# First head pairs of an attention + two-MLP kernel: who issues which load, k ahead of q, weight loads later, and w3 transposed as fp32r

## The chip, the cores and the metric

One core of a Trainium2 chip runs the kernel. The metric is device microseconds of one launch, the median of several runs.

## What is computed

Three stages in fp32, one after the other (cut from the reference; every weight is an input):

```python
# attention: q, k, v are (4, 8, 576, 64)
def rotate(x):
    x1, x2 = (x[..., :half], x[..., half:])
    return np.concatenate([x1 * cos - x2 * sin, x1 * sin + x2 * cos], axis=-1)
scores = scale * np.matmul(rotate(q), rotate(k).transpose(0, 1, 3, 2))
attn = softmax(scores)                 # max subtracted, 1e-09 added to the sum
x = np.matmul(attn, v)                 # then heads are merged: (2304, 512)

# first MLP: d_ff 1536
xn = x / rms * rms_g
x = (silu(xn @ w_gate) * (xn @ w_val)) @ w_out

# second MLP: d_ff 1024
h = (x @ w1) * (x @ w2) @ w3
out = h @ w_out2
```

## The kernel before, in words

Precision is kept by splitting: an fp32 value becomes a high part of type fp32r and a low part (value minus high part, also fp32r), and a product of two such values is three fp32r matmuls. ScalarE (ACT) makes the high part with a copy, VectorE (DVE) or GpSimd (POOL) subtracts it from the value for the low part.

**Attention** runs over 16 pairs of heads. For a pair, `load` (line 494) brings q and k into a tile `raw` of nine blocks per head: blocks 0 to 3 are q's rows 0 to 511, blocks 4 to 7 k's, block 8 holds the last 64 rows of both. `ra`, `rb`, `rc`, `rd` (lines 532 to 558) do the rotation: times cosine, the two half products with the sine (`rb` needs the negated sine, which ACT makes at line 880), and the sum, into `rot`. GpSimd does it for all pairs but the first, where VectorE does blocks 4 to 7 and 0 to 3 and GpSimd block 8. Three groups of transposes follow, `q2p` (k's blocks), `q1p` (q's) and `q0p` (block 8), line 591; for each, `q?h` copies the high part and `q?l` subtracts the low part into the tile `xy` (lines 595, 600). From `xy`, DMAs fill the stacks that the score matmuls read: `q2d` fills `ks` with four transfers (288 KB each), `q1d` fills `qs` with four (160 KB each), both through `move` (line 612). For the first pair part of the stacks is filled by copies and subtracts on the engines (lines 602, 889, 901).

A pair then goes through nine tiles of 128 query rows: `S` scores (line 660), `M` row maximum (665), `E` exponential (671), `T` transpose of the probabilities (677), `H` and `Lo` their split (681, 685), `LP`, `LH`, `LL` the same for the leftover columns (707, 711, 715), then `PV` (733), `OS` (738), `O` (747) and the scaled result `X`.

The order is written out by hand. `ORDER` gives each step a place inside a pair, in units of a ninth of a pair; pair p adds 9p; steps whose names begin with `q` or `v` are those of the next pair, and `ra` to `rd`, `lq`, `lv` those of the pair after it. `ONCE` gives single places: `WF.n` issues the load of weight unit n (512 KB, lines 405 and 407), `W0.n` to `W5.n` convert it (`W0` is an ACT instruction on the loaded tile, line 430; `W1` a DVE one, line 434). All steps are sorted by place, and each engine runs its own in that order, so an instruction that waits holds up all that follow it on its engine. DMAs are issued by SP (SyncE), in the same way in order. `WARM` counts filler transposes of the identity `idn` (line 877) between the first pair's transposes.

**The MLPs** are laid out by `Plan` (line 129): each operation has an estimated duration, operands and engine, and TensorE's order is the order of the program. `w3_trans(j)` (line 1541) transposes a part of w3, eight transposes of 128x128 for each of eight j, in two groups of four with a planned duration of 0.44; `w3_prod` multiplies the transposed part with the second `w_out`. Lines of other large products: 1305, 1452, 1561, 1619.

Of the kernel before, what the change touches and what calls it, by code (L numbers as in the profile page):

```python
# [30 lines left out]

ONCE = {"WF.0": 0.058, "WF.1": 0.481, "W0.0": 2.871, "W1.0": 9.2, "W2.0": 9.7, "W0.1": 7.205, "W3.0": 10.2,
# [8 lines left out]
WARM = (22, 18, 3, 26)  # L41
SEGS = ((0, 0, 4), (1, 0, 12), (0, 4, 12))
# [35 lines left out]
PRI = 100  # L78
Q_LATE = 0.023
LGROUPS = ((0, 1, 2, 3), (4,), (5, 6, 7, 8))  # L80
# [193 lines left out]
def kernel(  # L274
# [63 lines left out]

    idn = const.tile([128, 128], F32, name="idn")
    g_sb = const.tile([128, DM], F32, name="g")  # L340
# [153 lines left out]
    def load(p, t=None):  # L494
        raws[p] = t = raw_p.tile([128, 2, 9, D], F32, tag="raw", name="raw") if t is None else t
        nc.sync.dma_start(out=t[:, :, 4:8, :].rearrange("p h r d -> p h (r d)"), in_=main(k, p))
        if p == 0:
            nc.sync.dma_start(out=sin_sb[:, 1], in_=sin_t)
        nc.sync.dma_start(out=t[:, :, 0:4, :].rearrange("p h r d -> p h (r d)"), in_=main(q, p))
        if p == 0:  # L500
            nc.sync.dma_start(out=cos_sb[:, 0:4], in_=cos_t[:, 0:4])
        nc.sync.dma_start(out=t[64:128, :, 8, :], in_=left(k, p))
        nc.sync.dma_start(out=t[0:64, :, 8, :], in_=left(q, p))

# [77 lines left out]
    def qt(g):  # L582

        n = [1, 4, 4][g]
        r0 = [8, 0, 4][g]
        c = slice(*((0, 512) if g == 1 else (QW + LF, QW + S)))

        def qp(p):
            ps = ps_g.tile([128, 512], F32, tag="g", name="qtp")
            for i in range(n):  # L590
                nc.tensor.transpose(ps[:, i * 128:(i + 1) * 128], rots[p][:, r0 + i].rearrange("p h d -> p (h d)"), idn)  # L591
            qps[p, g] = ps if g else ps[:, 0:128].rearrange("p (a b) -> p a b", a=2)

        def qh(p):
            nc.scalar.copy(out=xs[:, c] if g else two(xs), in_=qps[p, g])

        def ql(p):
            hi, lo = (xs[:, c], ys[:, c]) if g else (two(xs), two(ys))
            ps = qps.pop((p, g))
            nc.vector.tensor_tensor(out=lo, in0=ps, in1=f(hi), op=ALU.subtract)  # L600
            if p == 0 and g == 1:
                nc.vector.tensor_tensor(out=qst[0][64:128, 0, 0:512], in0=ps[0:64], in1=f(hi)[0:64], op=ALU.subtract)

        for n_, fn in (("p", qp), ("h", qh), ("l", ql)):
            part[f"q{g}{n_}"] = fn
# [8 lines left out]
    @step  # L614
    def q1d(p):
        qs = qst[p % 2]
        sl = slice(0, 640)
        sa = sl
        if p == 0:
            sa = slice(512, 640)  # L620
        move([(qs[0:64, 0, sa], xs[0:64, sa]), (qs[64:128, 0, sa], ys[0:64, sa]),
              (qs[64:128, 1, sl], xs[64:128, sl]), (qs[0:64, 1, sl], ys[64:128, sl])])

    @step
    def q2d(p):
        new_ks(p)
        ks = stacks[p]
        sl = slice(QW, QW + S)
        move([(ks[a:a + 64, 2 * h:2 * h + 2], xy[64 * h:64 * h + 64, :, sl]) for h in range(p == 0, 2) for a in (0, 64)])

# [228 lines left out]
    nc.vector.memset(eps, 1e-9)  # L859
    make_identity(nc, idn)  # L860
    man = ExitStack()
    man.enter_context(tc.manual_schedule())
    nc.sync.dma_start(out=cos_sb[:, 4:9], in_=cos_t[:, 4:9])
    load(0)
# [15 lines left out]
    nc.scalar.mul(out=sin_sb[:, 0], in_=sin_sb[:, 1], mul=-1.0)  # L880
    for n, eng in ((slice(4, 8), nc.vector), (slice(8, 9), nc.gpsimd), (slice(0, 4), nc.vector)):
        for n_ in ("ra", "rb", "rc", "rd"):
            part[n_](0, eng, n)
    for n_ in ("ra", "rb", "rc", "rd"):
        part[n_](1)
    new_ks(0)

    def k_copy(eng, i, r):
        eng(out=stacks[0][r:r + 64, i], in_=xy[0:64, i, QW:QW + S])

    for i, n_ in enumerate(("q2p", "q0p", "q1p")):
        part[n_](0)
        warm(i + 1)
    for n_ in ("q2h", "q0h", "q2l", "q0l", "q2d"):
        part[n_](0)
    k_copy(nc.scalar.copy, 0, 0)
    for r in (0, 64):
        k_copy(nc.vector.tensor_copy, 1, r)
    part["q1h"](0), part["q1l"](0)
    k_copy(nc.scalar.copy, 0, 64)  # L900
    nc.scalar.copy(out=qst[0][0:64, 0, 0:512], in_=xs[0:64, 0:512])
    for n_ in ("q1d", "vh", "vl"):
# [801 lines left out]
```

## Time and profile before

| | us |
|---|---|
| median of 3 runs | 1057.66 (1057.07 to 1058.37) |
| the profiled execution | 1058.29 |
| its span, first to last instruction | 1056.4 |
| TensorE busy in it | 1039.7 (98%) |
| DVE, ACT, POOL busy | 782.3, 646.3, 356.2 |

The span is what the views below show; the profiled execution's time is 1.9 us more, which lies around the span. In the views PE is TensorE, PEld its weight loads, SPq the queue of SP. A busy PE may run at half clock: PEclk says what was granted, 1.00 for 2.4 GHz and 0.50 for 1.2.

### The profile page before, as it was taken

To read this page: it belongs to the slowest core of one execution; us is meant where nothing else is said; L and a number is where in the kernel's file an instruction comes from. 1 tells how busy PE (TensorE), PEld (TensorE's weight loads), DVE (VectorE), ACT (ScalarE), POOL (GpSimd) and SP (SyncE) were. 2 spreads that over 40 slices of the span, in tenths; PEclk is the share of its full clock that TensorE was granted. 3 is DMA by queue.
4 is the path that set the end of the run, shared out by engine and by line. 5 is a ranking of instruction groups with operands and counts; after the bars stand their busy time and mean duration, and the time that the engine had idled before them with its cause. 6 is when DMAs were issued, how large, how long until landed. Compare 5 with 4: busy or idle time off the path is not lost.

```text
span 1056.4 us, 19366 instructions
## 1 busy us (share of the span) xinstructions
PE 1039.7 (98%) x6849; PEld 1024.1 (97%) x6849; DVE 782.3 (74%) x1382; ACT 646.3 (61%) x1433; POOL 356.2 (34%) x479
## 2 busy tenths in 40 slices
PE   8899999999999999999999999999999999999998
PEld 7799999999999999999999999999999999989998
DVE  7899999999987965878787777443675574774663
ACT  5799999899977655457666675422554444454330
POOL 7779788889610002532222230001521110000000
PEclk9999999999999999999999999999999999999999
DMA  7778876768669876369988967561352326751751
GB/s 197 163 204 204 223 184 177 195 184 197 175 212 307 284 259 231 95 213 341 312 299 266 310 231 233 166 214 48 107 205 81 125 76 214 276 197 53 269 217 61
DMA packets 124864, 211.36 MB, mean 200 GB/s; under 512 B 19040, under 2 KB 71776, under 8 KB 123232
## 3 DMA queue, kind: packets, MB, share of 16 engines
q1 hardware_dynamic: 124768, 210.14, 63.8%
q8 instruction: 54, 0.88, 0.3%
q14 instruction: 42, 0.34, 0.1%
HBM read 117.62 MB, written 63.96 MB: 172 GB/s over the span
## 4 chain that ended last, share of the span: by engine, by line
PE 94%; DVE 2%; DMA 2%; POOL 1%; issue 1%; SPq 0%; ACT 0%; DVEq 0%; POOLq 0%
PE ps L1305 33%; PE ps L1452 9%; PE mm L1062 9%; PE ps L1619 9%; PE s L660 7%; PE pv L733 7%; PE tp L677 6%; PE acc L1088 5%; PE ps L1561 4%; PE lp L707 1%; PE op L747 1%; PE qtp L591 1%; DMA ks<-xy 1%; PE ps L1548 1%; PE xp L1189 1%; DMA raw<-in_q_dram 1%
## 5 line engine op out<-in xcount | busy, mean ns | idle before, releaser
L995 DVE TENSOR_TENSOR v<-v 128x256 fp32r<-128x256 f32 (+7 forms) x436 | 277.5, 666 | 115.1 <-ACT v L989 103.0
L1305 PE MATMUL ps<-v 128*128 128x384 f32 x2016 | 350.0, 334 | 0.0
L1305 PEld LDWEIGHTS ps<-v 128*128 128x128 f32 x2016 | 349.4, 188 | 0.0
L989 ACT CAST v<-v 128x256 fp32r<-128x256 f32 (+4 forms) x372 | 196.0, 556 | 149.4 <-PE ps L1305 38.8
L995 POOL TENSOR_TENSOR v<-v 128x256 f32<-128x256 f32 (+1 forms) x120 | 113.7, 963 | 427.6 <-DMA v<-wsG 159.6
L995 DVE TENSOR_TENSOR v<-ps,v 128x384 f32<-128x384 f32 (+3 forms) x154 | 84.3, 567 | 86.4 <-PE ps L1305 46.7
L989 ACT COPY v<-ps 128x384 f32<-128x384 f32 (+1 forms) x126 | 60.2, 478 | 113.0 <-PE ps L1305 57.0
L660 PE MATMUL s<-ks,qs 128*128 128x288 f32 x640 | 120.4, 314 | 7.2 <-DMA ks<-xy 3.1
L665 DVE TENSOR_REDUCE nm<-s 128x1 f32<-128x576 f32 x144 | 108.0, 750 | 11.4 <-PE s L660 9.7
L671 ACT ACTIVATE p<-s,nm 128x576 f32<-128x576 f32 x144 | 107.4, 746 | 11.2 <-DVE nm L665 10.5
L1062 PE MATMUL mm<-v 128*128 128x384 f32 x576 | 104.2, 335 | 0.1
L1062 PEld LDWEIGHTS mm<-v 128*128 128x128 f32 x576 | 99.9, 188 | 0.4 <-DVE pt L685 0.4
L1452 PE MATMUL ps<-v 128*128 128x384 f32 x576 | 100.0, 334 | 0.0
L1452 PEld LDWEIGHTS ps<-v 128*128 128x128 f32 x576 | 99.9, 188 | 0.0
L660 PEld LDWEIGHTS s<-ks,qs 128*128 128x128 f32 x640 | 89.9, 190 | 9.9 <-issue 4.9
L685 DVE TENSOR_TENSOR pt<-tp,pt 128x512 fp32r<-128x512 f32 x144 | 94.7, 682 | 1.2 <-ACT pt L681 0.6
L1619 PEld LDWEIGHTS ps<-v 128*128 128x128 f32 x756 | 90.9, 192 | 0.1
L1619 PE MATMUL ps<-v 128*128 128x256 f32 x756 | 90.9, 283 | 0.0
L677 PE MATMUL tp<-idn,p 128*128 128x128 f32 x576 | 82.7, 276 | 1.5 <-DVE x L773 0.7
L681 ACT CAST pt<-tp 128x512 fp32r<-128x512 f32 x144 | 82.3, 585 | 1.5 <-PE tp L677 0.7
L733 PE MATMUL pv<-pt,vs 128*128 128x288 f32 x512 | 80.9, 300 | 0.1
L677 PEld LDWEIGHTS tp<-idn,p 128*128 128x128 f32 x576 | 68.1, 142 | 3.5 <-PE s L660 1.3
(118 smaller groups left out, 1262.0 us busy)
## 6 DMA issues: line engine op xcount, KB each, us to landing
ks<-xy SPq DMA_DIRECT2D x62, 288.0 KB, 4.9
v<-in_moe_w_dram SPq DMA_DIRECT2D x32, 512.0 KB, 6.0
v<-uD SPq DMA_DIRECT2D x12, 1344.0 KB, 7.3
v<-in_moe_w_out_dram SPq DMA_DIRECT2D x20, 512.0 KB, 6.4
qs<-xy SPq DMA_DIRECT2D x62, 160.0 KB, 2.8
uG<-v SPq DMA_DIRECT2D x24, 384.0 KB, 4.1
v<-uG SPq DMA_DIRECT2D x24, 384.0 KB, 3.7
uD<-v SPq DMA_DIRECT2D x12, 768.0 KB, 3.6
```

The source lines that it names most:

```text
L660: nc.tensor.matmul(ps[:, hf, 0:HS], lhsT=l, rhs=r_[:, hf * HS:(hf + 1) * HS], start=(i == 0), stop=(i == n - 1))
L665: nc.vector.tensor_reduce(out=nm, in_=s_ps[p, t][:, :, 0:HS], axis=AX.XY, op=ALU.max, negate=True)
L671: nc.scalar.activation(out=pp.rearrange("p (a b) -> p a b", a=2), in_=s_ps.pop((p, t))[:, :, 0:HS], func=AF.Exp, bias=s_max.pop((p, t)), s ...
L677: nc.tensor.transpose(ps[:, c, :], p_sb[p, t][:, LF + c * 128:LF + (c + 1) * 128], idn)
L685: lastins["dve"] = nc.vector.tensor_tensor(out=lo, in0=src, in1=f(hi), op=ALU.subtract)
L733: nc.tensor.matmul(ps[:, 0:HS], lhsT=l.rearrange("p s d -> p (s d)"), rhs=r, start=(i == 0), stop=(i == 8))
L989: return plan("ACT", act_us(n), lambda: nc.scalar.copy(out=o(), in_=i()), rd, wr)
L995: lambda: eng.tensor_tensor(out=o(), in0=x(), in1=y(), op=op), rd, wr)
L1062: nc.tensor.matmul(p_, lhsT=w.ap[:, a, s, c * 128:(c + 1) * 128], rhs=x.ap[:, b_, c, :], start=(j == 0), stop=(j == 3 * KC - 1))
L1305: nc.tensor.matmul(p_(), lhsT=w[i].ap[:, a, c * 128:(c + 1) * 128], rhs=x[i].ap[:, r, c], start=(first and ch != 1 and n == 0), stop=(n == 5),
L1452: nc.tensor.matmul(ac[o][ch][0](), lhsT=w.ap[:, a, o * 128:(o + 1) * 128], rhs=u.ap[:, b_, ch], start=(j == 0 and s == 0), stop=(j == NF - ...
L1619: nc.tensor.matmul(p_()[:, k * 256:(k + 1) * 256], lhsT=u.ap[:, a, UOP[i], o * 128:(o + 1) * 128], rhs=w.ap[:, b_], start=(g == 0 and s == ...
```

## The change

- Opening loads. The first half of the cosines that is needed, the sine, and the first pair's two 64-row pieces are issued by ACT instead of SP. SP issues the first pair's k, then q, then the rest of the cosines, and for the second pair k, the two pieces, then q.
- The identity is made in a scratch tile and copied by ACT into an fp32r tile `idr`; `idn` is the fp32 view of it.
- First pair: the rotation's order is `ra`, `rc`, `rb`, `rd`. k's low part is subtracted from PSUM directly into both halves of the stack (`k_lo`), for the 512 main columns and the 64 left ones apart; the high part is copied there by ACT (`k_hi`). The DMAs to the other head's stack are split in the same way (`k_move`), and the last DMAs to `qs` are issued in another order. `WARM` has smaller numbers.
- Second pair: GpSimd rotates blocks 4 to 8 first, then 0 to 3. Its `q2` and `q0` steps stand ahead of S2 and near S3 of the first pair, with `q2d` ahead of E2; its `q1` steps stand at 1.2 to 1.42.
- The first two weight loads move from 0.058 and 0.481 to 1.6 and 1.7, and `W0.0` from 2.871 to 5.8.
- `w3_trans` transposes as fp32r, with `idr`.

```diff
-ONCE = {"WF.0": 0.058, "WF.1": 0.481, "W0.0": 2.871, "W1.0": 9.2, "W2.0": 9.7, "W0.1": 7.205, "W3.0": 10.2,
+ONCE = {"WF.0": 1.6, "WF.1": 1.7, "W0.0": 5.8, "W1.0": 9.2, "W2.0": 9.7, "W0.1": 7.205, "W3.0": 10.2,
-WARM = (22, 18, 3, 26)
+WARM = (20, 15, 3, 16)
-Q_LATE = 0.023
+FIRST = {"q2p": -0.34, "q0p": -0.335, "q2h": -0.2, "q0h": -0.19, "q2l": -0.06, "q0l": -0.05, "q2d": -0.03,
+    "q1p": 1.2, "q1h": 1.25, "q1l": 1.4, "q1d": 1.42}
...
-    idn = const.tile([128, 128], F32, name="idn")
+    idr = const.tile([128, 128], F32R, name="idr")
+    idn = f(idr)
...
     def load(p, t=None):
+        first = p == 0
+        if first:
+            nc.scalar.dma_start(out=cos_sb[:, 4:9], in_=cos_t[:, 4:9])
         nc.sync.dma_start(out=t[:, :, 4:8, :].rearrange("p h r d -> p h (r d)"), in_=main(k, p))
-        if p == 0:
-            nc.sync.dma_start(out=sin_sb[:, 1], in_=sin_t)
-        nc.sync.dma_start(out=t[:, :, 0:4, :].rearrange("p h r d -> p h (r d)"), in_=main(q, p))
-        if p == 0:
+        if first:
+            nc.scalar.dma_start(out=sin_sb[:, 1], in_=sin_t)
+        if p != 1:
+            nc.sync.dma_start(out=t[:, :, 0:4, :].rearrange("p h r d -> p h (r d)"), in_=main(q, p))
+        if first:
             nc.sync.dma_start(out=cos_sb[:, 0:4], in_=cos_t[:, 0:4])
-        nc.sync.dma_start(out=t[64:128, :, 8, :], in_=left(k, p))
-        nc.sync.dma_start(out=t[0:64, :, 8, :], in_=left(q, p))
+        eng = nc.scalar if first else nc.sync
+        eng.dma_start(out=t[64:128, :, 8, :], in_=left(k, p))
+        eng.dma_start(out=t[0:64, :, 8, :], in_=left(q, p))
+        if p == 1:
+            nc.sync.dma_start(out=t[:, :, 0:4, :].rearrange("p h r d -> p h (r d)"), in_=main(q, p))
...
-make_identity(nc, idn)
+ident = p_p.tile([128, S], F32, tag="p", name="ident")[:, 0:128]
+make_identity(nc, ident)
+nc.scalar.copy(out=idr, in_=ident)
-nc.sync.dma_start(out=cos_sb[:, 4:9], in_=cos_t[:, 4:9])
...
-    for n_ in ("ra", "rb", "rc", "rd"):
-        part[n_](1)
+    for n in (slice(4, 9), slice(0, 4)):
+        for n_ in ("ra", "rb", "rc", "rd"):
+            part[n_](1, nc.gpsimd, n)
...
+    def k_lo(c, r):
+        src = qps[0, 2] if c is K_MAIN else qps[0, 0][:, 1, 0:64]
+        nc.vector.tensor_tensor(out=ks[r:r + 64, 1, c[0]:c[1]], in0=src[0:64], in1=f(xs)[0:64, QW + c[0]:QW + c[1]], op=ALU.subtract)
...
-    for i, n_ in enumerate(("q2p", "q0p", "q1p")):
+    for i, n_ in enumerate(("q2p", "q1p", "q0p")):
         part[n_](0)
         warm(i + 1)
-    for n_ in ("q2h", "q0h", "q2l", "q0l", "q2d"):
+    ps_k = qps[0, 2]
+    part["q2h"](0)
+    for r in (0, 64):
+        k_hi(K_MAIN, r)
+    nc.vector.tensor_tensor(out=ys[:, QW + LF:QW + S], in0=ps_k, in1=f(xs)[:, QW + LF:QW + S], op=ALU.subtract)
+    k_move(K_MAIN)
+    for r in (0, 64):
+        k_lo(K_MAIN, r)
+    part["q1h"](0)
+    part["q0h"](0)
+    nc.scalar.copy(out=qst[0][0:64, 0, 0:512], in_=xs[0:64, 0:512])
+    nc.vector.tensor_tensor(out=qst[0][64:128, 0, 0:512], in0=qps[0, 1][0:64], in1=f(xs)[0:64, 0:512], op=ALU.subtract)
+    for r in (0, 64):
+        k_hi(K_LEFT, r)
+        k_lo(K_LEFT, r)
+    for n_ in ("q0l", "q1l"):
         part[n_](0)
-    k_copy(nc.scalar.copy, 0, 0)
-    for r in (0, 64):
-        k_copy(nc.vector.tensor_copy, 1, r)
-    part["q1h"](0), part["q1l"](0)
-    k_copy(nc.scalar.copy, 0, 64)
-    nc.scalar.copy(out=qst[0][0:64, 0, 0:512], in_=xs[0:64, 0:512])
+    k_move(K_LEFT)
...
-                at(9 * p + t + (Q_LATE if p == 0 and n_[0] == "q" else 0), part[n_], p + d)
+                at(9 * p + (FIRST.get(n_, t) if p == 0 else t), part[n_], p + d)
...
-                    nc.tensor.transpose(p_()[:, c * 128:(c + 1) * 128], src.ap[:, c * 128:(c + 1) * 128], idn)
+                    nc.tensor.transpose(p_()[:, c * 128:(c + 1) * 128].bitcast(F32R), src.ap[:, c * 128:(c + 1) * 128].bitcast(F32R), idr)
```

## Rows read from the trace of the kernel before

**Rows 1.** The page: busy time and share by engine; shares of the chain that ended last.
```profile
PE 1039.7 (98%) x6849; PEld 1024.1 (97%) x6849; DVE 782.3 (74%) x1382; ACT 646.3 (61%) x1433; POOL 356.2 (34%) x479
...
PE 94%; DVE 2%; DMA 2%; POOL 1%; issue 1%; SPq 0%; ACT 0%; DVEq 0%; POOLq 0%
```

**Rows 2.** Stretches: length, busy us of each engine, granted clock, DMA share, GB/s.
```profile
20.00:30.00 10.00, 8.07 (x59) 7.10 (x59) 9.04 (x15) 9.30 (x24) 10.00 (x15) 1.00 0.99 248
...
29.00:32.00 3.00, 0.04 (x1) 0.00 (x0) 0.54 (x1) 1.68 (x4) 2.42 (x3) 1.00 1.05 231
...
34.00:36.00 2.00, 2.00 (x11) 1.98 (x11) 1.44 (x2) 1.49 (x5) 0.23 (x1) 0.50 1.02 322
...
40.00:44.00 4.00, 3.69 (x30) 3.28 (x30) 4.00 (x8) 3.13 (x7) 4.00 (x4) 1.00 0.20 45
44.00:50.00 6.00, 5.44 (x43) 5.18 (x43) 5.94 (x10) 4.85 (x13) 5.93 (x9) 1.00 0.82 180
...
50.00:100.00 50.00, 50.00 (x411) 49.75 (x410) 48.96 (x87) 47.11 (x117) 39.09 (x57) 1.00 0.81 205
...
890.00:960.00 70.00, 70.00 (x370) 62.12 (x369) 53.15 (x92) 37.22 (x70) 0.00 (x0) 1.00 0.55 199
```

**Rows 3.** Order of time, opening: start, us, engine, line, operation [idle before <-releaser].
```profile
0.74 1.28 ACT L871 ACT_TABLE_LOAD   x1 [0.74 <-PEq L1690]
...
1.36 4.77 PE L877 MATMUL warm<-idn 128*128 128x128 f32 x22 [1.36 <-POOL idn masks.py:199]
...
3.95 0.62 SPq L503 DMA_DIRECT2D raw<-in_q_dram  x1
...
10.87 2.37 DVE L889 CAST ks<-xy 64x576 fp32r<-64x576 f32 x2
...
14.83 1.28 PE L660 MATMUL s<-ks,qs 128*128 128x288 f32 x8 [1.01 <-DVE qs L602]
```

**Rows 4.** Chain that ended last, in order of time: start, us, what.
```profile
24.83 7.19 DMA ks<-xy
...
32.15 0.76 PE s L660 x4
...
37.36 0.44 PE tp L677 x4
```

**Rows 5.** Order of time, first and second pair.
```profile
9.79 3.14 POOL L538 TENSOR_TENSOR rot<-xr,cos 128x384 f32<-128x384 f32 x3
...
15.90 0.54 SPq L496 DMA_DIRECT2D raw<-in_k_dram  x1
...
16.40 2.92 POOL L558 TENSOR_TENSOR rot<-rot,rtmp 128x384 f32<-128x384 f32 x3
...
17.31 1.52 PE L660 MATMUL s<-ks,qs 128*128 128x288 f32 x8 [1.20 <-ACT p L671]
...
18.42 0.60 SPq L407 DMA_DIRECT2D v<-in_moe_w_gate_dram  x1
...
25.11 0.70 ACT L430 ACTIVATE v<-v 128x512 f32<-128x512 f32 x1
...
27.93 0.74 ACT L671 ACTIVATE p<-s,nm 128x576 f32<-128x576 f32 x1 [0.32 <-DVE nm L665]
...
32.76 0.70 PE L707 MATMUL lp<-idn,p 128*64 128x128 f32 x4
```

**Rows 6.** DMA issues at 17.9 to 21 us: KB each, median us to landing.
```profile
v<-in_moe_w_gate_dram SPq DMA_DIRECT2D x1, 512.0 KB, 4.8
v<-in_moe_w_val_dram SPq DMA_DIRECT2D x1, 512.0 KB, 7.7
```

**Rows 7.** Groups by line and shape: count | busy us, mean ns of one.
```profile
L1305 PE MATMUL ps<-v 128*128 128x384 f32 x2016 | 350.0, 334 | 0.0
...
L1619 PE MATMUL ps<-v 128*128 128x256 f32 x756 | 90.9, 283 | 0.0
...
L1548 PE MATMUL ps<-idn,v 128*128 128x128 f32 x64 | 8.3, 272 | 0.0
```

More of the change, by code (lines that the diff above doesn't have):

```diff
@@ L600, in ql @@
             nc.vector.tensor_tensor(out=lo, in0=ps, in1=f(hi), op=ALU.subtract)
-            if p == 0 and g == 1:
-                nc.vector.tensor_tensor(out=qst[0][64:128, 0, 0:512], in0=ps[0:64], in1=f(hi)[0:64], op=ALU.subtract)
         for n_, fn in (("p", qp), ("h", qh), ("l", ql)):
@@ L620, in q1d @@
             sa = slice(512, 640)
-        move([(qs[0:64, 0, sa], xs[0:64, sa]), (qs[64:128, 0, sa], ys[0:64, sa]),
-              (qs[64:128, 1, sl], xs[64:128, sl]), (qs[0:64, 1, sl], ys[64:128, sl])])
+        m = [(qs[0:64, 0, sa], xs[0:64, sa]), (qs[64:128, 0, sa], ys[0:64, sa]),
+             (qs[64:128, 1, sl], xs[64:128, sl]), (qs[0:64, 1, sl], ys[64:128, sl])]
+        move([m[i] for i in (2, 0, 3, 1)] if p == 0 else m)
     @step
@@ L628, in q2d @@
         sl = slice(QW, QW + S)
-        move([(ks[a:a + 64, 2 * h:2 * h + 2], xy[64 * h:64 * h + 64, :, sl]) for h in range(p == 0, 2) for a in (0, 64)])
+        if p:
+            move([(ks[a:a + 64, 2 * h:2 * h + 2], xy[64 * h:64 * h + 64, :, sl]) for h in range(2) for a in (0, 64)])
     def new_ks(p):
@@ L881, with k_hi, k_move @@
     for n, eng in ((slice(4, 8), nc.vector), (slice(8, 9), nc.gpsimd), (slice(0, 4), nc.vector)):
+        for n_ in ("ra", "rc", "rb", "rd"):
+            part[n_](0, eng, n)
+    for n in (slice(4, 9), slice(0, 4)):
         for n_ in ("ra", "rb", "rc", "rd"):
-            part[n_](0, eng, n)
-    for n_ in ("ra", "rb", "rc", "rd"):
-        part[n_](1)
+            part[n_](1, nc.gpsimd, n)
     new_ks(0)
-    def k_copy(eng, i, r):
-        eng(out=stacks[0][r:r + 64, i], in_=xy[0:64, i, QW:QW + S])
-    for i, n_ in enumerate(("q2p", "q0p", "q1p")):
+    ks = stacks[0]
+    K_MAIN, K_LEFT = (LF, S), (0, LF)
+    def k_hi(c, r):
+        nc.scalar.copy(out=ks[r:r + 64, 0, c[0]:c[1]], in_=xs[0:64, QW + c[0]:QW + c[1]])
+    def k_lo(c, r):
+        src = qps[0, 2] if c is K_MAIN else qps[0, 0][:, 1, 0:64]
+        nc.vector.tensor_tensor(out=ks[r:r + 64, 1, c[0]:c[1]], in0=src[0:64], in1=f(xs)[0:64, QW + c[0]:QW + c[1]], op=ALU.subtract)
+    def k_move(c):
+        move([(ks[a:a + 64, 2:4, c[0]:c[1]], xy[64:128, :, QW + c[0]:QW + c[1]]) for a in (0, 64)])
+    for i, n_ in enumerate(("q2p", "q1p", "q0p")):
         part[n_](0)
         warm(i + 1)
-    for n_ in ("q2h", "q0h", "q2l", "q0l", "q2d"):
-        part[n_](0)
-    k_copy(nc.scalar.copy, 0, 0)
-    for r in (0, 64):
-        k_copy(nc.vector.tensor_copy, 1, r)
-    part["q1h"](0), part["q1l"](0)
-    k_copy(nc.scalar.copy, 0, 64)
-    nc.scalar.copy(out=qst[0][0:64, 0, 0:512], in_=xs[0:64, 0:512])
+    ps_k = qps[0, 2]
[6 more added lines that the diff above has]
+        k_lo(K_MAIN, r)
+    qps.pop((0, 2))
+    part["q1h"](0)
[6 more added lines that the diff above has]
+    for n_ in ("q0l", "q1l"):
+        part[n_](0)
+    k_move(K_LEFT)
     for n_ in ("q1d", "vh", "vl"):
```

## The prediction, made before the changed kernel ran

> **What bounds the kernel now.** I read four views in this order. First the page's busy shares and the chain that ended last [rows 1]: TensorE is busy 1039.7 of 1056.4 us and carries 94% of the chain, so time is won only by giving TensorE work earlier or by making its work shorter. Then the stretches [rows 2]: from 50 us on TensorE is full (50.00 of 50), and full again in 890 to 960 us (70.00 of 70). Its idle time lies in the opening and in the first two head pairs: in 29 to 32 us it works 0.04 of 3 us, in 34 to 36 us it is busy but at a granted clock of 0.50 (1.2 instead of 2.4 GHz, just after that idle time), and in 40 to 50 us it idles 0.31 + 0.56 = 0.87 us. Then the opening [rows 3]: the first score matmul starts at 14.83 us; before that TensorE mostly runs filler transposes. Last the chain and the order of time through the first two pairs [rows 4, 5]: the score matmuls of the second pair wait until 32.15 us for its k stack, whose transfer (7.19 us in the chain) stands behind two weight loads of 512 KB [rows 5, 6].
>
> So two places can give something: whatever delays the point from which TensorE stays full (about 33 us), and TensorE's own work later, which w3's transposes are part of.
>
> **The change, part by part.**
>
> *w3's transposes.* There are 64, TensorE is full there, so each nanosecond counts fully. An f32 transpose of 128 columns takes 0.44/4 = 0.110 us from start to start [rows 4]. No fp32r matmul of 128 columns is in the trace. Matmuls on fp32r tiles cost 350.0/2016 = 0.1736 us at 384 columns and 90.9/756 = 0.1202 at 256 [rows 7]: 0.0534 less for 128 fewer, so 0.067 at 128. That saves 64 x 0.043 = 2.8 us. Bounds: no better than this line, and no worse than a 256-column fp32r matmul (0.120), which loses 0.6 us. I take 2.8, since the row at 256 columns lies on the line. The planner's 0.44 us for four is unchanged, so its order stays. A row shows a mean of 272 ns for one w3 transpose [rows 7], but starts lie 0.110 us apart. The Trainium skill, "TensorE: Matmul & The Clock Gate", Part 4: PE-mode transpose, puts a 128x128 bf16 transpose at about 275 ns, most of it the latency of reading SBUF; if that latency were the cost here, the type would change nothing and this term would be 0.
>
> *Opening loads.* Seven loads of the first pair were issued by SP one behind the other, the last at 3.95 us [rows 3]; four of them now go by ACT. ACT's first instruction is now the copy of the identity, and the table load that takes ACT from 0.74 to 2.02 us [rows 3] goes ahead of it. If ACT's loads wait for that, its cosines are issued 1.3 us later than today; if not, about when SP issues them today. So the k rotation ends between 1 us earlier and 1.5 us later. The filler transposes also wait for that copy: 20 x 0.217 us (4.77/22 [rows 3]) from about 2.3 us end near 6.7. The rule that speaks against this part is in the Trainium skill, "DMA: Bandwidth & Descriptors", Issuing engines are not separate DMA queues: issuing from several engines saves only issue time. The rows cannot show it, since only SP issues here; by it the 1008 KB land no earlier.
>
> *VectorE in the opening.* The two 64x576 copies of k's low part (2.37 us [rows 3]) go; the subtracts now write the stacks. Ahead of the first scores VectorE then does one 128x512 subtract, three of 64x512 and two of 64x64, some 0.69 x 4 + 0.3 x 2 = 3.4 us in place of 4.7 (two of 0.69, one of 0.29, the copies, and 0.69 for q). With the loads' uncertainty the first score matmul moves from 14.83 to 12.6 to 13.9 us; I take 13.2.
>
> *Second pair's k first.* GpSimd rotates the second pair from 9.79 to 19.32 us [rows 5]; doing k and the left rows first (5 of 9 blocks) has them ready at 9.8 + 5/9 x 9.5 = 15.1 (14.0 to 16.7 with the loads). New wait: their transposes now stand ahead of S2 on TensorE, so S2 waits for GpSimd: about 16.0 instead of 17.31. Behind it stand M2, E2 and the rest. SP issues the k stack's four transfers near 18 instead of 24.2, ahead of q's and of the weights, so it lands near 24 instead of 32.0: this wait is gone.
>
> *Weights later.* What is late next is the first weight load. SP's order is now: third pair's loads (576 KB), k stack (4 x 288), q stack (640), second pair's v (320), g (256), then WF.0 (512). WF.0 stood ahead of the k stack and was issued at 18.42 [rows 5]; now it stands behind q1d, which waits for q1l near 21.3, then 4 + 3 + 1 issues of about 0.6 us: not before 26. And it is queued behind 2944 KB. From SP's arrival at the third pair's loads (about 15.8 us; 15.90 today) 3456 KB must pass. Rates: 248 GB/s (242 KB/us) in the full stretch 20 to 30 us [rows 2]; 3392 KB from 16.5 to 32.0 us, 219 KB/us, for today's mix up to the k stack [rows 4]. I take 230: 15.0 us, so from 16.2 to 31.2, landed at 31.7. Bounds: 31.0 at 242, and 35 if transfers with short rows go as slowly as today's, without the two fast weight loads (1024 KB in 3 us): (3392 - 1024)/12.5 = 189 KB/us for 2944 KB.
>
> W0.0 is a ScalarE instruction that reads this load. It moves from 2.871 to 5.8 in the order, right behind E7 and ahead of E8. E7 started at 27.93 [rows 5] and ended at 28.8, 11.4 us behind S2; without W0.0's 0.70 us in between [rows 5] it ends at 16.0 + 10.7 = 26.7 (25.7 to 28.2). So ScalarE waits at W0.0 from about 27 to 31.7, and behind it are queued E8, OS00, W0.1, LH8 and the second pair's first exponentials. TensorE finishes PV00 and the second pair's first scores (near 28) and then needs E8 for LP8. W0.0 0.70 + E8 0.75 + hand-overs 0.1: LP8 at 33.25. Today it starts at 32.76 [rows 5], with 0.53 us of scores (S0) still to its side that are done already in the new order, so the equal point is 33.3. **The stall is nearly as long as before, with another owner.** The half clock stays too, since idle time of over 3 us comes before it in both. Left of the gain: about 0.1 us, and the 0.87 us of idle in 40 to 50 us [rows 2], which I expect to go since q, k and v of the second pair and q of the third are then ready sooner: 1.0 us.
>
> Sum: 1.0 + 2.8 = 3.8 us. The profiled execution took 1058.29 (span 1056.4, 1.9 around it), 0.6 above the median of 1057.66; it would go to 1054.5, the median to **1053.9**.
>
> **The rivals.**
>
> *No wait at W0.0.* If the weights land by 28, the second pair's scores start near 28 instead of 32.15 (4.1 us), the half clock over some 3.3 us goes (1.7 us), with the 0.9 and 2.8: 9.5 us, 1048.2. Against it: 3456 KB in 12 us are 288 KB/us, above any stretch shown; for it, that ScalarE may come later than I think, which shortens the wait. Partly so, it gives 1050.
>
> *Weights land far later (slower).* The place is again W0.0, the price 1 us per us. With 1.0 and 2.8 in hand the change turns slower if WF.0 lands after 35.5, 3.8 us behind my figure. For it: the row rate of 189 KB/us gives 35, and a k rotation 1.5 us late moves SP's start as well. That gives 1057.5 to 1060.5, say 1059.
>
> *fp32r transposes cost as much as f32.* For it: no row at 128 columns; one f32 transpose and one fp32r matmul have like durations, 272 and 283 ns [rows 7]. Then 1053.9 + 2.8 = 1056.7.
>
> **How the numbers follow.** My forecast (ScalarE waits at W0.0, the load landing at 31 to 33.5, w3 saves 2.8: 1052.5 to 1056) 0.52; no or little wait (1047 to 1051) 0.20; weights far later 0.13; w3 without gain 0.15. The range leaves out about a tenth on each side: the better half of the second case below, the worst of the third above: 1048.2 to 1058.6. A measurement tells about 0.2% (2.1 us) from no change. Below 1055.5: 0.42 of the first case, all of the second and 0.02 of the last, 0.64. Above 1059.8: 0.07 of the third, 0.02 of the fourth (with the bound of -0.6), 0.09. The rest is 0.27.
>
> **What would show it.** In the new profile: the first scores near 13 and S2 near 16; the k stack's transfers issued near 18 and landed near 24, no TensorE wait for them; ScalarE idle for 3 to 6 us before line 430 with the load of w_gate as releaser, near 27 to 32; TensorE waiting for E8 before the transposes of line 707; a low clock behind that; groups of eight w3 transposes 0.34 us shorter. I am wrong if ScalarE does not wait at line 430, if GpSimd has k later than 16.7, or if w3's starts stay 0.110 us apart.

## The result, and the profile after

The changed kernel takes **1063.86 us** (median of 6, 1062.17 to 1065.11) beside 1057.37 for the kernel before on the same chip (median of 6, 1055.93 to 1059.67): a ratio of 1.0059, interval 1.0043 to 1.0076. It is slower by 6.5 us, where 1053.9 us was predicted. The profiled execution took 1062.61 us with a span of 1060.8 us, 4.4 us more than the span before. Lines of the kernel have moved by 2 to 31: the scores are now at 669 (660 before), the exponential at 680 (671), the left probabilities' transposes at 716 (707), the weight arithmetic that begins with W0.0 at 432 (430), w3's transposes at 1579 (1548).

The page of the changed kernel, busy time and the shares of the chain that ended last, answering [rows 1]:

```profile
PE 1036.8 (98%) x6834; PEld 1020.8 (96%) x6834; DVE 779.4 (73%) x1384; ACT 647.7 (61%) x1436; POOL 353.8 (33%) x475
...
PE 89%; DMA 3%; POOL 3%; DVE 3%; issue 1%; SPq 1%; ACT 1%; DVEq 0%; POOLq 0%
```

TensorE is busy 2.9 us less and carries 89% of the chain instead of 94%: its work didn't grow, it waits more. For what, two views say: the list of waits in the first 70 us (engine, line, what it waited for: us in total, times, longest), and the chain in order of time from 26 to 38 us.

```profile
ACT v L432 <- DMA v<-in_moe_w_gate_dram: 8.4, 1, 8.4
...
PE lp L716 <- ACT p L680: 8.1, 1, 8.1
```

```profile
26.55 0.59 SPq L516
...
29.19 6.38 DMA v<-in_moe_w_gate_dram
...
36.15 0.82 ACT p L680 x2
```

One wait, of ScalarE for the first weight load, lasts 8.4 us, and TensorE's 8.1 us hang on it: the exponential (E8) stands behind W0.0 on ScalarE, the transposes of line 716 (LP8) need E8. The chain goes on backwards from the load into SP's queue (26.55): the load wasn't only slow, it was issued late. The stretches (length, busy us of PE, PEld, DVE, ACT, POOL, each with its count of instructions, then granted clock, DMA share, GB/s) answer [rows 2]:

```profile
29.20:32.00 2.80, 0.00 (x0) 0.00 (x0) 0.23 (x1) 0.00 (x0) 2.80 (x4) 0.76 0.70 106
32.00:34.00 2.00, 0.00 (x0) 0.00 (x0) 0.00 (x0) 0.00 (x0) 1.73 (x3) 0.50 0.99 280
...
37.00:41.00 4.00, 3.99 (x19) 3.97 (x20) 2.13 (x3) 3.73 (x10) 2.88 (x6) 0.51 0.10 31
...
50.00:100.00 50.00, 49.19 (x401) 48.35 (x399) 48.92 (x85) 45.99 (x116) 33.39 (x48) 1.00 0.80 205
```

Before, TensorE idled some 3 us ahead of 32.15 and worked from 33 to about 36.3 us at half clock. Now it idles from 29 to 37 us and then works some 4 us at half clock (0.51 in 37 to 41 us). Behind it, in 50 to 100 us, it loses 0.81 us where it lost none.

The order of time (start, us, engine, line, operation), answering [rows 3] and [rows 5]:

```profile
0.74 0.43 ACTq L500 DMA_DIRECT2D cos<-in_cos_dram  x1
...
1.20 0.44 ACTq L503 DMA_DIRECT2D sin<-in_sin_dram  x1
...
1.68 1.28 ACT L871 ACT_TABLE_LOAD   x1 [1.68 <-PEq L1721]
...
3.32 4.06 PE L887 MATMUL warm<-idr 128*128 128x128 f32 x20 [3.32 <-ACT idr L871]
...
11.83 1.30 PE L669 MATMUL s<-ks,qs 128*128 128x288 f32 x8
...
13.13 1.53 POOL L567 TENSOR_TENSOR rot<-rot,rtmp 128x640 f32<-128x640 f32 x1
...
15.25 1.30 PE L669 MATMUL s<-ks,qs 128*128 128x288 f32 x8
...
18.68 3.80 SPq L619 DMA_DIRECT2D ks<-xy  x4
22.58 3.92 SPq L619 DMA_DIRECT2D qs<-xy  x4
...
26.34 0.74 ACT L680 ACTIVATE p<-s,nm 128x576 f32<-128x576 f32 x1 [0.40 <-DVE nm L674]
...
27.86 0.77 PE L669 MATMUL s<-ks,qs 128*128 128x288 f32 x4 [0.51 <-DMA qs<-xy]
...
29.19 0.43 SPq L409 DMA_DIRECT2D v<-in_moe_w_gate_dram  x1
...
35.59 0.65 ACT L432 ACTIVATE v<-v 128x512 f32<-128x512 f32 x1 [8.42 <-DMA v<-in_moe_w_gate_dram]
...
37.01 0.42 PE L716 MATMUL lp<-idr,p 128*64 128x128 f32 x1 [8.05 <-ACT p L680]
```

The opening does what it was changed for: the first scores start 3.0 us sooner (11.83 against 14.83), the second pair's at 27.86 instead of 32.15. But its k and q stacks take SP from 18.68 to 26.50, and the weight load is issued at 29.19. Four of the eight stack issues took some 0.6 us each. The four from 20.00 to 25.21 took 0.88, 1.56, 1.30 and 1.24, as the spread of the two stacks' issues shows (shortest, median and longest in ns):

```profile
L619 SPq DMA_DIRECT2D ks<-xy x4: 613/744/1562, 18.7 to 20.9; - x4
L619 SPq DMA_DIRECT2D qs<-xy x4: 588/920/1296, 22.6 to 25.9; - x4
```

They weren't waiting for q: ScalarE had written its high part by 20.16 us and VectorE the low part by 20.88. The weight load's transfer, in the DMA view of 29.2 to 32 us (packets in flight; issue: KB, us to landing), answering [rows 6]:

```profile
DMA packets 377, 0.30 MB, mean 106 GB/s; under 512 B 245, under 2 KB 271, under 8 KB 377
...
v<-in_moe_w_gate_dram SPq DMA_DIRECT2D x1, 512.0 KB, 6.4
```

By count most of these packets are short; they are v's 64-row pieces, and v has landed by 30.3 us. What fills the stretch behind that is g, as the view of 30.3 to 32 us and g's issue show:

```profile
DMA packets 104, 0.18 MB, mean 105 GB/s; under 512 B 6, under 2 KB 28, under 8 KB 104
```

```profile
g<-in_moe_rms_g_dram SPq DMA_DIRECT2D x1, 256.0 KB, 5.5
```

Here 76 of 104 packets have 2 KB or more, which of the transfers on the way only g's rows have (one row of 2 KB, read once for each of 128 partitions). g landed at 34.0 us. Why its rows go so slowly here isn't shown. The weight load takes 6.4 us from issue to landing instead of 4.8.

At the far end, w3's transposes (TensorE's order of time around two successive groups of eight, then the page's group over all 64: count | busy us, mean ns of one), answering [rows 7]:

```profile
922.77 0.80 PE L1579 MATMUL ps<-idr,v 128*128 128x128 f32 x8
...
928.97 0.80 PE L1579 MATMUL ps<-idr,v 128*128 128x128 f32 x8
```

```profile
L1579 PE MATMUL ps<-idr,v 128*128 128x128 f32 x64 | 6.4, 243 | 0.0
```

From one group to the next it is 6.20 us (928.97 - 922.77), 6.33 before. From the first transpose to the last the stretch shrank by 1.4 us, not 2.8.

**Where the 4.4 us came from.** The first output transposes (line 747 before, 756 now) start 4.4 us later:

```profile
50.14 0.60 PE L747 MATMUL op<-idn,osb 128*128 128x128 f32 x4
```

```profile
54.52 0.60 PE L756 MATMUL op<-idr,osb 128*128 128x128 f32 x4
```

So as much as the whole 4.4 us is lost by then. On the way to the fifth pair's output 0.7 more are lost (123.7 against 118.6), up to w3 another 0.7 (901.3 against 895.5), and w3 gives 1.4 back: 5.8 - 1.4 = 4.4.

### The profile page after: what moved, and what is told of

Same layout as the page of the kernel before. It is cut to its first block, busy times and chain, and to the rows that moved or that the text cites. A ratio compares the mean times of both kernels' runs of the same rounds, so it can differ in the third digit from the quotient of the medians.

```text
span 1060.8 us, 19348 instructions
## 1 busy us (share of the span) xinstructions
PE 1036.8 (98%) x6834; PEld 1020.8 (96%) x6834; DVE 779.4 (73%) x1384; ACT 647.7 (61%) x1436; POOL 353.8 (33%) x475
## 4 chain that ended last, share of the span: by engine, by line
PE 89%; DMA 3%; POOL 3%; DVE 3%; issue 1%; SPq 1%; ACT 1%; DVEq 0%; POOLq 0%
PE ps L1336 33%; PE ps L1483 9%; PE mm L1093 9%; PE ps L1650 9%; PE s L669 6%; PE pv L742 5%; PE acc L1119 5%; PE tp L686 4%; PE ps L1592 4%; PE qtp L600 1%; PE lp L716 1%; PE op L756 1%; POOL rtmp L553 1%; DVE pt L694 1%; POOL rot L547 1%
## 5 line engine op out<-in xcount | busy, mean ns | idle before, releaser
L686 PE MATMUL tp<-idr,p 128*128 128x128 f32 x576 | 82.9, 276 | 1.0 <-DVE pt L694 0.5
L742 PE MATMUL pv<-pt,vs 128*128 128x288 f32 x512 | 80.9, 300 | 0.1
L742 PEld LDWEIGHTS pv<-pt,vs 128*128 128x128 f32 x512 | 70.9, 188 | 0.3 <-DVE pt L694 0.3
```

The source lines that it names most:

```text
L686: nc.tensor.transpose(ps[:, c, :], p_sb[p, t][:, LF + c * 128:LF + (c + 1) * 128], idn)
L742: nc.tensor.matmul(ps[:, 0:HS], lhsT=l.rearrange("p s d -> p (s d)"), rhs=r, start=(i == 0), stop=(i == 8))
```

## The experiments

The theory after the result: in SP's queue the second pair's stacks, v and g now stand ahead of the first weight load, which comes too late for W0.0's new place, and everything behind W0.0 on ScalarE waits. The rivals: another part of the change costs the time (the opening, fp32r, k's order), or the weight load is late by its own place in the plan whatever stands ahead. Each ratio is to the kernel before on the same chip, whose median lay between 1057.37 and 1058.95 us; it can differ a little from the quotient of the two medians.

| kernel | us | ratio (interval) |
|---|---|---|
| weight loads' new places alone | 1066.20 | 1.0072 (1.0052 to 1.0092) |
| changed kernel | 1063.86 | 1.0059 (1.0043 to 1.0076) |
| changed, weights at their places of before | 1061.45 | 1.0035 (1.0019 to 1.0051) |
| only the opening's change and w3's | 1061.11 | 1.0028 (1.0014 to 1.0042) |
| changed, weights ahead of v and g | 1059.55 | 1.0010 (0.9995 to 1.0026) |
| w3's change alone | 1057.67 | 0.9990 (0.9972 to 1.0007) |
| before, weights spread over three pairs | 1056.91 | 1.0001 (0.9985 to 1.0018) |
| before, weights read late | 1056.81 | 0.9987 (0.9973 to 1.0001) |
| changed, weights read late | 1055.24 | 0.9971 (0.9956 to 0.9985) |
| changed, weights behind the fourth pair | 1054.88 | 0.9959 (0.9938 to 0.9981) |
| changed, weights spread over three pairs | 1053.88 | 0.9959 (0.9944 to 0.9973) |

**Take the reader away, keep the load.** In the changed kernel the first weight arithmetic moves from place 5.8 to 12 and on; the loads stay.

```diff
-ONCE = {"WF.0": 1.6, "WF.1": 1.7, "W0.0": 5.8, "W1.0": 9.2, "W2.0": 9.7, "W0.1": 7.205, "W3.0": 10.2, "W1.1": 10.9,
+ONCE = {"WF.0": 1.6, "WF.1": 1.7, "W0.0": 12.0, "W1.0": 12.2, "W2.0": 12.4, "W0.1": 13.0, "W3.0": 12.6, "W1.1": 13.2,
```

> The changed kernel, with the arithmetic on the first two weight units (W0 to W3) at 12 to 13.2 instead of 5.8 to 10.9, so that ScalarE reaches the loads after they have landed (35.6 us). Loads stay where they are. Theory A (the loss is ScalarE held at W0.0, with E8 and LP8 behind it): the wait of 8.4 us at the weight's first instruction goes, LP8 starts at 28 to 29.5 instead of 37.0, the clock stays at 2.4 GHz there, and the time is 1052 to 1055. Theory B (the new order of the second pair's k and q, or the opening, costs the time, and the wait at W0.0 only covers it): TensorE stalls on something else before 37 us and the time stays at 1061 to 1064.

Measured 1055.24 us, some 9 us below the changed kernel by the ratios (0.9971 against 1.0059). Its order of time on TensorE, two pieces of its chain on VectorE, and the stretch of 30 to 40 us:

```profile
28.75 0.77 PE L669 MATMUL s<-ks,qs 128*128 128x288 f32 x4 [0.53 <-DMA qs<-xy]
29.36 0.60 PE L716 MATMUL lp<-idr,p 128*64 128x128 f32 x4
...
44.05 0.60 PE L756 MATMUL op<-idr,osb 128*128 128x128 f32 x4
45.79 1.29 PE L742 MATMUL pv<-pt,vs 128*128 128x288 f32 x8 [1.15 <-DVE pt L694]
```

```profile
43.15 0.91 DVE v L440
...
44.08 0.97 DVE v L445
```

```profile
30.00:40.00 10.00, 10.00 (x84) 9.89 (x83) 9.63 (x17) 9.84 (x24) 4.82 (x10) 1.00 0.91 232
```

The wait is gone, TensorE is full at full clock where it had stood still, and the first output starts at 44.05, 10.5 us before the changed kernel's and 6.1 before the old one's. But only some 3 us are left of the 6.1: the second pair's output is at 64.2 instead of 67.2, the fifth's at 115.8 instead of 118.6. The second pair takes 20.2 us instead of 17.1, and TensorE waits at 45.79 for VectorE, which between two probability subtracts (line 694) does the weight arithmetic of lines 436 to 445. VectorE (the third busy time of these lines) has hardly any room left: from 30 us to the fifth pair's output it works 83.90 of 85.80 us here, and 82.75 of 88.60 before:

```profile
30.00:115.80 85.80, 83.81 (x673) 81.67 (x672) 83.90 (x142) 78.36 (x194) 70.02 (x100) 1.00 0.81 205
```

```profile
30.00:118.60 88.60, 85.58 (x681) 84.44 (x682) 82.75 (x142) 78.44 (x194) 69.85 (x100) 0.98 0.78 194
```

Much of its work had been done in the very stall that was removed.

**The weight loads' places alone**, in the kernel before.

```diff
-ONCE = {"WF.0": 0.058, "WF.1": 0.481, "W0.0": 2.871, "W1.0": 9.2, ...
+ONCE = {"WF.0": 1.6, "WF.1": 1.7, "W0.0": 5.8, "W1.0": 9.2, ...
```

> The kernel before with one part of the change alone: the weight loads at 1.6 and 1.7 and W0.0 at 5.8. Theory A: the k stack no longer has the two 512 KB loads ahead of it and lands near 27 to 28 instead of 32.0, but W0.0 waits for a load issued near 29 to 31 and landing at 34 to 37, so ScalarE waits 5 to 8 us at line 430 and the time is 1060 to 1063. Theory B: this part alone is harmless or a gain (1053 to 1058).

Measured 1066.20 us, the slowest of all. Its waits and the piece of its chain:

```profile
ACT v L430 <- DMA v<-in_moe_w_gate_dram: 9.6, 1, 9.6
...
PE lp L707 <- ACT p L671: 9.3, 1, 9.3
```

```profile
31.74 6.36 DMA v<-in_moe_w_gate_dram
```

This one line of the change costs as much as the whole change, within the intervals. The load is issued at 31.74 here and at 29.19 in the changed kernel, and takes the same 6.4 us.

**The weights at their places of before**, in the changed kernel (the same line, the other way round).

```diff
-ONCE = {"WF.0": 1.6, "WF.1": 1.7, "W0.0": 5.8, "W1.0": 9.2, ...
+ONCE = {"WF.0": 0.058, "WF.1": 0.481, "W0.0": 2.871, "W1.0": 9.2, ...
```

> The changed kernel with the weight loads and W0.0 back at 0.058, 0.481 and 2.871. SP then issues the two weight loads between the second pair's k stack and its q stack, near 22.5 us. Theory A: ScalarE is held at W0.0 again, but for 1 to 4 us only (load landed near 27 to 28, wanted at 24), and the q stack behind the weights lands near 31, so that the second pair's scores start near 31: 1055 to 1059. Theory B: about the time of the changed kernel, 1061 to 1064.

Measured 1061.45 us, slower than the 1055 to 1059 expected. Now the load is issued at 22.87 us, between the k and the q stack, and ScalarE waits for it 5.0 us at the earlier place of W0.0. The scores of the first pair's last part then wait for ScalarE:

```profile
31.02 1.33 PE L669 MATMUL s<-ks,qs 128*128 128x288 f32 x4 [5.99 <-ACT p L680]
```

With k first, W0.0's old place is too early as well. The stall stays, with the same releaser.

**The load ahead of v and g**, in the changed kernel: only the place in SP's queue differs.

```diff
-    at(1.5, load_v, 1, vt)
-    at(1.5, nc.sync.dma_start, g_sb, ...)
+    at(1.8, load_v, 1, vt)
+    at(1.8, nc.sync.dma_start, g_sb, ...)
```

> The changed kernel with the second pair's v and g issued behind the first two weight loads (1.8 instead of 1.5). In the changed kernel four issues of v and g stand ahead of WF.0 (26.55 to 29.14 us), and from 29.2 to 32 us the DMA engines move only 106 GB/s. If the place in SP's queue sets the landing, WF.0 is issued near 26.5, lands near 30 to 31.5, ScalarE's wait at W0.0 falls from 8.4 to 3 to 5 us and the time from 1063.9 to 1059 to 1061. If ScalarE's late W0.0 is bound by something else (the weight load's own 6.4 us from issue to landing), it falls by no more than 2.6 us of earlier issue, or not at all: 1061 to 1064.

Measured 1059.55 us. The load is issued at 26.51 us, 2.7 sooner; ScalarE waits 3.5 us instead of 8.4, and TensorE resumes 4.9 us sooner than in the changed kernel:

```profile
32.07 0.42 PE L716 MATMUL lp<-idr,p 128*64 128x128 f32 x1 [2.97 <-ACT p L680]
```

The load itself took 4.1 us instead of 6.4, so it landed at 30.62 us, 4.9 sooner (chain, in order of time):

```profile
26.51 4.11 DMA v<-in_moe_w_gate_dram
```

Same work, same readers, another order of issue: the queue sets the landing, by the time of issue (2.7 us) and by what stands right ahead (2.3 us), and the landing sets the time.

**Only the opening** (with w3): weights at their places of before, and the first pairs' steps too.

```diff
-                at(9 * p + (FIRST.get(n_, t) if p == 0 else t), part[n_], p + d)
+                at(9 * p + t + (0.023 if p == 0 and n_[0] == "q" else 0), part[n_], p + d)
```

> The changed kernel with the second pair's q and k steps and the weight loads back at the places of before, so that the opening, GpSimd's k first and w3 as fp32r are left. First scores near 11.8 us as in the changed kernel (14.83 before). If the second pair's k stack (behind third pair's loads, 1 MB of weights and the q stack) sets the time from which TensorE is full, its transfers end near 31 to 32 as before and the three us of the opening come to nothing: 1055.5 to 1057.5, 1.0 of it w3. If they carry through, 1053 to 1054.5.

Measured 1061.11 us: the opening by itself makes the kernel slower. The first scores start at 12.10 us, 2.7 sooner, but the second pair's still wait for k:

```profile
32.53 1.30 PE L669 MATMUL s<-ks,qs 128*128 128x288 f32 x4 [4.65 <-DMA ks<-xy]
```

In the kernel before they start at 32.15 [rows 4] after a wait of 3.11 us. What was won became idle time, 1.5 us longer, and the clock was at half from about 31 to 38 us instead of 33 to 36.3: the first output starts at 52.6, 2.5 us later than before. The k stack's transfers are issued from 23.93, against 24.17 before, hardly sooner. Nor did the loads bring the first scores forward: VectorE's first rotation, which waits for the first pair's k, starts at 4.34 us here and at 4.19 before.

```profile
4.34 0.69 DVE L547 TENSOR_TENSOR rot<-raw,cos 128x512 f32<-128x512 f32 x1 [2.94 <-DMA raw<-in_k_dram]
```

```profile
4.19 0.69 DVE L538 TENSOR_TENSOR rot<-raw,cos 128x512 f32<-128x512 f32 x1 [2.79 <-DMA raw<-in_k_dram]
```

The last piece of the first pair's q, issued by ACT at 2.46 us in the changed kernel and by SP at 3.95 before, landed 5.0 us later there and 3.2 before, at 7.4 and 7.2. The opening's gain arises behind the loads, and no run separates its parts. That the loads land no sooner agrees with the Trainium skill, "DMA: Bandwidth & Descriptors", Issuing engines are not separate DMA queues, by which a second issuing engine saves only the time to issue.

**w3 alone**, in the kernel before (with the fp32r identity that it needs).

```diff
-nc.tensor.transpose(p_()[:, c * 128:(c + 1) * 128], src.ap[:, c * 128:(c + 1) * 128], idn)
+nc.tensor.transpose(p_()[:, c * 128:(c + 1) * 128].bitcast(F32R), src.ap[:, c * 128:(c + 1) * 128].bitcast(F32R), idr)
```

> The kernel before with w3's 64 transposes as fp32r alone (and the identity copied by ScalarE for it). By the changed kernel's trace a round of 24 matmuls and 8 transposes takes 6.20 instead of 6.33 us, so 8 such rounds give 1.0 us: 1056.4 to 1056.8, which a measurement can hardly tell from no change. By the prediction's 2.8 us: 1054.6. If the identity's later copy (fillers start at 3.3 instead of 1.4 us) moves the opening, it shows as a first score matmul later than 14.83 us.

Measured 1057.67 us, ratio 0.9990 (0.9972 to 1.0007): a gain of 1.4 us fits, and so does none. The identity's copy moved the opening little: the first scores start at 14.99 us, 14.83 before. The next run measures the transposes by themselves.

**w3's transposes eight times over**, in the changed kernel, the first group of four in f32 and the second in fp32r. This adds 448 transposes (not the number that the expectation names); the last of each eight is what is used.

```diff
-                for c in range(4):
-                    nc.tensor.transpose(p_()[:, ...].bitcast(F32R), src.ap[:, ...].bitcast(F32R), idr)
+                for c in [i for _ in range(8) for i in range(4)]:
+                    if h: nc.tensor.transpose(p_()[:, ...].bitcast(F32R), src.ap[:, ...].bitcast(F32R), idr)
+                    else: nc.tensor.transpose(p_()[:, ...], src.ap[:, ...], idn)
```

> The changed kernel with every group of four w3 transposes done eight times over, the first of each two groups in f32, the second in fp32r: 32 in a row of each, so that starts can be read without the neighbours. By the line through fp32r matmuls of 256 and 384 columns an fp32r transpose starts every 0.067 us, by the changed kernel's rounds (6.33 to 6.20 us for 24 matmuls and 8 transposes) every 0.090 to 0.095, and an f32 one every 0.110. The other 1792 transposes make the kernel some 170 us longer; its total says nothing here.

Measured 1107.76 us (one run). TensorE around the first groups, f32 at line 1583 and fp32r at 1580:

```profile
902.39 3.66 PE L1583 MATMUL ps<-idr,v 128*128 128x128 f32 x32
905.80 2.90 PE L1580 MATMUL ps<-idr,v 128*128 128x128 f32 x32
908.53 14.80 PE L1336 MATMUL ps<-v 128*128 128x384 f32 x84
```

From start to start an f32 transpose takes (905.80 - 902.39)/32 = 0.107 us and an fp32r one (908.53 - 905.80)/32 = 0.085: 0.0213 saved, 1.4 us for 64. The 448 added ones make 224 x 0.192 = 43.0 us, and 1063.9 + 43.0 = 1106.9.

**The weights read late in the kernel before**: its plan as in the first experiment.

```diff
-ONCE = {"WF.0": 0.058, "WF.1": 0.481, "W0.0": 2.871, "W1.0": 9.2, "W2.0": 9.7, "W0.1": 7.205, "W3.0": 10.2, "W1.1": 10.9,
+ONCE = {"WF.0": 1.6, "WF.1": 1.7, "W0.0": 12.0, "W1.0": 12.2, "W2.0": 12.4, "W0.1": 13.0, "W3.0": 12.6, "W1.1": 13.2,
```

> The kernel before with the first two weight loads at 1.6 and 1.7 and their arithmetic at 12 to 13.2, nothing else of the change. If the 1 MB ahead of the stacks was what held the second pair's k, its scores start near 29 instead of 32.15 without any of the other parts, nobody waits for the weights, and the time is 1054 to 1056, near the 1055.2 of the changed kernel with the arithmetic late. If the opening and k ahead of q are needed for it, it stays at 1057 to 1058.

Measured 1056.81 us, 0.9987 (0.9973 to 1.0001), above the 1054 to 1056 expected. Without a line of the opening or of k's order the second pair's scores start at 29.30 us (27.86 in the changed kernel):

```profile
29.30 0.76 PE L660 MATMUL s<-ks,qs 128*128 128x288 f32 x4 [0.41 <-DMA ks<-xy]
```

So the wait of [rows 4] came from the two weight loads ahead of the k stack, and 1 MB out of the way takes it away. That 2.9 us sooner there (29.30 against 32.15) brings only some 1.4 us at the end, if any, shows again that the gain is taken back behind it (GpSimd here waits 6.8 us for the third pair's q, and TensorE is busy 9.48 of 10 us in 40 to 50).

**The weights behind the fourth pair's loads**, loads at 10.0 and arithmetic from 14.0 on, in the changed kernel.

```diff
-ONCE = {"WF.0": 1.6, "WF.1": 1.7, "W0.0": 5.8, "W1.0": 9.2, "W2.0": 9.7, "W0.1": 7.205, "W3.0": 10.2, "W1.1": 10.9,
+ONCE = {"WF.0": 10.0, "WF.1": 10.05, "W0.0": 14.0, "W1.0": 14.3, "W2.0": 14.6, "W0.1": 15.2, "W3.0": 14.9, "W1.1": 15.5,
```

> The changed kernel with the first two weight loads behind the fourth pair's q and k (10.0 and 10.05) and their arithmetic at 14 to 15.5. With the arithmetic alone moved the kernel ran at 1055.2, and TensorE still idled 1.6 us in 40 to 50 us, with GpSimd waiting 4.7 us for the fourth pair's load that stands behind the weights. Theory: that load lands some 3 us sooner, the idle time in 40 to 50 us falls to under 0.8 us, time 1053 to 1055. Rival: the weights' 1 MB then collides with the third pair's stacks, which need the same queue near 37 to 44 us, and the gain is lost again: 1055 to 1058.

Measured 1054.88 us, 0.9959 (0.9938 to 0.9981). The second pair again gives back most of the gain: the outputs are at 43.6 and 64.7 us. These are read in the slowest of its twelve runs (1060.34 us), so what they are worth in the others isn't shown.

**The weights spread over three pairs**, so that VectorE never has two of them close together.

```diff
+ONCE = {"WF.0": 10.0, "WF.1": 10.05, "W0.0": 13.0, "W1.0": 13.6, "W2.0": 15.2, "W0.1": 15.0, "W3.0": 19.4, "W1.1": 16.9, ..., "W2.1": 21.4,
```

> The changed kernel with the first two weight loads behind the fourth pair's q and k (10.0, 10.05) and their arithmetic spread out (13.0 to 21.4, at least a sixth of a pair between two VectorE instructions). With that arithmetic within 1.2 places the first pair's output came 6 us earlier than before the change, but the second pair took 20.2 to 21.1 us instead of 17.1, with VectorE full and three weight instructions of 0.9 to 1.4 us in the chain. Theory (VectorE's weight instructions in a row gave the gain back): the second pair takes 17.1 to 18 us and the time is 1051.5 to 1053.5. Rival (the third pair's stacks are late whatever stands on VectorE): the second pair still takes 20 us, 1054.5 to 1056.

Measured 1053.88 us, 0.9959 (0.9944 to 0.9973), the lowest median, but not below the kernel before it by more than the interval. Its profiled execution is the slowest of its six (1057.84 us). There the second to fourth pair take 18.6, 18.7 and 21.4 us (outputs at 43.6, 62.2, 80.9 and 102.3), with waits on VectorE in each: spread out, the loss is no smaller. That clumped weight arithmetic alone takes the gain back isn't confirmed. How much of it is VectorE's capacity and how much the raw loads' arrival stays open.

**The same places in the kernel before.**

```diff
-ONCE = {"WF.0": 0.058, "WF.1": 0.481, "W0.0": 2.871, "W1.0": 9.2, ...
+ONCE = {"WF.0": 10.0, "WF.1": 10.05, "W0.0": 13.0, "W1.0": 13.6, ..., "W2.1": 21.4,
```

> The kernel before with the same places of the first two weight units, and nothing else of the change: no opening, no k ahead of q, w3 as f32. If the 1 MB of weights ahead of the second pair's stacks was the whole stall, the scores of the second pair start near 29.3 instead of 32.15 and the time is 1053.5 to 1055.5 (1 to 2 us above the changed kernel with the same places, 1.4 us of that w3). If the opening and k ahead of q carry through, it lies 3 to 5 us above that kernel.

Measured 1056.91 us, 1.0001 (0.9985 to 1.0018). With the same places of the weights, the rest of the change (opening, k first, w3) is worth 1.0001 - 0.9959 = 0.4%, about 4 us; with those of the first experiment 0.9987 - 0.9971 = 0.2%, which lies within the intervals. In each, 1.4 us are w3's by the run with the transposes eight times over. So with the weights spread out the opening and k first are a gain, though its size is known only roughly.

## Why the prediction was wrong

**The mechanism was right, the size of one term wasn't.** ScalarE waits at W0.0 for w_gate, TensorE behind E8 before LP8, at half clock afterwards: each was named, and each is in the trace. The failed step is the landing of the first weight load, which I took from the bytes ahead of it and one rate: predicted at 31.7 us (bounds 31.0 and 35), measured at 35.57 (29.19 + 6.38 in the chain).

*The rate.* SP reached the third pair's loads at 16.15 us, as predicted (16.2), but the 3456 KB that I counted from there took 19.4 us, 178 KB/us, where I had taken 230 and a lower bound of 189. I had misread the row behind it. The 32.0 us of [rows 4] are the landing of the k stack's second transfer, not of its last. Its third and fourth, issued at 25.48 and 26.89, took 8.0 and 7.8 us (us to landing, shortest, median and longest of the four):

```profile
DMA to landing us min/median/max: 6.6/7.5/8.0
```

Up to the landing of the last, at 34.7, the 3392 KB took 18.2 us, 186 KB/us and not 219. By 186 the load lands at 35.2.

*The count.* The engines weren't slow on the whole. From 16.15 us to the landing they moved 4.34 MB, 4238 KB, which is 219 KB/us:

```profile
DMA packets 3721, 4.34 MB, mean 224 GB/s; under 512 B 831, under 2 KB 2768, under 8 KB 3720
```

Some 780 KB of this I had not counted. Transfers issued behind the weight load moved in part before it was complete: from 29.19 us on 1.45 MB (1416 KB) went by, of which v, g and the load itself can be 1088 KB at most.

*The place in the queue.* I wrote "not before 26" for the load's issue, with 0.6 us for each ahead of it; it came at 29.19, and the four longer issues of the stacks make 2.6 us of that. With v and g behind it the load lands at 30.62. So the 576 KB of v and g, 2.5 us at my rate, cost 4.9 us: 2.4 of the 3.9 us by which I was wrong. The other 1.4 arise ahead of them. These three are views of the same 3.9 us and don't add up.

From the landing on the sum held: LP8 at 37.01, 1.44 us behind it (1.55 predicted).

**The slower rival is what happened**, at its place and by its mechanism, though its 1057.5 to 1060.5 was too low as well. Its turning point of 35.5 was too kind, since it counted on 1.0 and 2.8 us in hand that weren't there. From the forecast (3.8 us faster) to the profile (4.4 slower) there are 8.2 us: 3.8 from LP8 (37.01 instead of 33.25); 1.6 up to the first output, namely the 0.9 us of idle time that I expected to go and that stayed (TensorE works 9.18 of 10 us in 44.4 to 54.4, 9.13 in 40 to 50 before), and 0.7, of which the half clock, some 4 us long instead of 3.3, explains 0.3 or 0.4; 1.4 between the first output and w3; and 1.4 of w3. By the medians the loss is 2 us more than by the two profiles.

**The opening** came out better than predicted and was worth nothing here. The scores started at 11.83 (12.6 to 13.9 predicted), GpSimd had the second pair's k at 14.66 (15.1), S2 started at 15.25 (16.0), E7 ended at 27.17 (26.7). ScalarE reached W0.0 sooner than a load issued at 29.19 could land, and only waited longer.

**w3.** The saving is real and half as large: 0.021 us a transpose, not 0.043. I drew a line through two fp32r matmuls of 256 and 384 columns down to 128; the measured 0.085 lies between that line's 0.067 and the bound of 0.120. The rival that the type changes nothing is out: the mean of one fell too, from 272 to 243 ns. The duration in that row is still not the price, since starts lie 0.085 us apart.

**The chances.** 0.13 for the rival that came true was too little. That its landing bound of 35 came close is partly luck: it rests on the same misread 32.0, and on slow transfers with short rows, while the stretches that hold the stacks went faster than its 189 KB/us, at 206 and 239 GB/s (201 and 233 KB/us, in 18.6 to 22.5 and 22.5 to 26.5 us). Against the rival without a wait I wrote that no stretch shows 288 KB/us; [rows 2] has one of 322 GB/s, 314 KB/us, in 34 to 36 us.

## What to carry to other kernels

When a load is moved behind others in a queue, price the issues ahead one by one where the same issues stand in the trace, take a rate only up to the landing of the last transfer that it counts, and allow for bytes issued behind the load that move before it is complete; and look at which instruction reads it, on which in-order engine, and what stands behind that one. A wait that goes away uncovers the engine that had worked in its shade: its busy share over the stretch, here VectorE's 82.75 of 88.60 us, bounds what can be kept. Move the reader together with the load, or later: that alone turned 0.6% slower into 0.3% faster here.

## What the runs showed of the hardware that was not expected

ScalarE's own DMA issues went ahead of its first computation's table load: they went out at 0.74 and 1.20 us, and the table load moved from 0.74 to 1.68, so that the identity's copy and with it the filler transposes started at 3.32 us.

Most issues of a stack's moves on SP took 0.5 to 0.6 us (the four of the second pair's q in the kernel before 504 to 588 ns), but some far more: up to 1.36 us for the k stack before and 1.56 in the changed kernel. A sum over four issues hides this. What makes them long, no run separates.

A 512 KB load took 4.8 us from issue to landing before, 6.3 to 6.4 in the changed kernel and the other three runs in which v and g stood right ahead of it (the reader late, in either kernel, and the places alone), and 4.1 where v and g stood behind it.
